# Attention output: the two halves of an accumulator added by GpSimd instead of VectorE

## The chip, the cores and the metric

The kernel runs on one core of a Trainium2 chip. The core has five engines that each run their own queue of instructions in order and wait for one another through semaphores: TensorE (PE; its weight loads are shown apart as PEld), VectorE (DVE), ScalarE (ACT), GpSimd (POOL) and SyncE (SP), which here issues DMAs. Matrix products land in PSUM; everything else lives in SBUF. The metric is the device time of one execution in microseconds (us).

## What is computed

An attention layer, a dense layer with a rational activation and a gated mixture of eight expert layers, one behind the other, in float32. Only the attention matters here:

```
B, H, S, D = q.shape                      # 2, 8, 768, 64
q_bits = (einsum('bhsd,dk->bhsk', q, proj) > 0)     # 6 bits; k_bits likewise
mask = q_bucket[:, :, :, None] == k_bucket[:, :, None, :]
scores = where(mask, q @ k.T / sqrt(D), -1e9)
attn = exp(scores - max) / (sum + 1e-9)
out = attn @ v                            # (b, s, h*64 + d) is the input of the next layer
```

## The kernel before

The program has an attention stage (to about 288 us), then the dense layer, then the experts. Precision is kept by splitting each float32 operand into a high half (rounded to the type that TensorE multiplies fast) and a low half, the rest; products are made of the halves.

The attention stage handles 16 heads (two batches of eight), each in three **groups** of 256 rows: 48 groups, `gi` from 0 to 47. The loop at the end of the listing runs over them with lags: in a turn it emits the scores of group `it`, the transposes of group `it - 2`, the products with v of group `it - 3`, and for a head's first two groups the preparation of the next head. Emission order is not the order of execution: a scheduler moves instructions within each engine's queue, by its own reckoning of what is ready, so every engine's order can change when one instruction changes. In a queue nothing overtakes.

The steps of a group, by name and line:

- `scores`: TensorE writes `s` (L277, L278); VectorE copies it to `e` and takes the row minimum of the negated scores (L285); ScalarE takes the exponential in place (L286).
- `norm`: VectorE makes the reciprocal row sums `rs` (L291, L292); GpSimd multiplies `e` by them, two tiles of 128x768 (L294). This is called the normalisation below.
- `trans`: TensorE transposes `e` into PSUM tiles `pt` (L308), which wait for L294; ScalarE copies them out as high halves `pth` (L106), VectorE makes the low halves `ptl` (L109).
- `values`: TensorE multiplies `pth` and `ptl` by `sv`, which holds v's high half in 64 columns and its low half in 64 more (L323). The accumulator `av` therefore has two halves in partitions 0 to 63 and 64 to 127 that must still be added. Before, ScalarE copies the lower one out to `avt`, and VectorE adds it to the upper one, read from PSUM, and writes 64 rows of `xp` (L334). `xp` collects two heads: an even head its rows 0 to 63, an odd head rows 64 to 127.
- Behind an odd head's group GpSimd splits 128x256 of `xp` into `xh` (L100) and `xl` (L103), the input of the dense layer.

For the next head GpSimd also splits v, q and k into `sv`, `sq`, `sk` (L100 and L103, 128x384 each); `sv` has three buffers. The tiles `av`, `pt`, `tp` and `hp` share four PSUM banks (tag "b"), so a bank must be read out before TensorE can use it again.

Beside attention the first weights of the dense layer are narrowed from 64-bit floats, eight of them in this stage. For one weight VectorE runs L180 to L183, GpSimd L170 (a clamp), L186 (an addition) and L103 (the low half, `wa` or `wb`), ScalarE L169 and a copy (L106) between L186 and L103.

Of the kernel before, what the change touches and what calls it, by code (L numbers as in the profile page):

```python
# [14 lines left out]
F32 = mybir.dt.float32  # L15
# [6 lines left out]
ALU = mybir.AluOpType  # L22
# [13 lines left out]
def kernel(  # L36
# [16 lines left out]
    pe, act, dve, pool, sp = nc.tensor, nc.scalar, nc.vector, nc.gpsimd, nc.sync  # L53
# [5 lines left out]
    P = 128  # L59
# [29 lines left out]
    def bank(name):  # L89
        return ps.tile([P, 512], F32, tag="b", bufs=4, name=name)  # L90
# [4 lines left out]
    def split(eng_hi, eng_lo, hi, lo, src):  # L95
        eng_hi(hi, src)
        eng_lo(lo, src, hi)
# [7 lines left out]
    def act_copy(o, src):  # L105
        act.activation(o, src, AF.Copy)  # L106
# [6 lines left out]
    ap = qkv_pool_stack.enter_context(tc.tile_pool(name="attn", bufs=2))  # L113
# [200 lines left out]
    def values(gi):  # L314
        i, g = divmod(gi, G)
        b, h = heads[i]
        sv = st[i][4]
        th, tl = pts.pop(gi)
        es.pop(gi)
        av = bank("av")  # L320
        for n, src in enumerate((th, tl)):
            for c in range(C):
                pe.matmul(av[:, 0:2 * P], lhsT=sv[:, c], rhs=src[:, c],  # L323
                          start=n == 0 and c == 0, stop=n == 1 and c == C - 1)
        if h % 2 == 0:
            if g == 0:
                xp[i] = ap.tile([P, S], F32, tag="xp", name="xp")
            x = xp[i]
        else:
            x = xp[i - 1]  # L330
        tmp = ap.tile([64, 2 * P], F32, tag="avt", name="avt")
        act_copy(tmp, av[64:128, 0:2 * P])
        r0 = (h % 2) * 64
        dve.tensor_tensor(x[r0:r0 + 64, g * 2 * P:(g + 1) * 2 * P], av[0:64, 0:2 * P], tmp, ALU.add)  # L334
        if h % 2:
            c0 = b * S + g * 2 * P
            tt, c0 = divmod(c0, 512)
            cs = slice(c0, c0 + 2 * P)
            split(pool_hi, pool_lo, xh[tt][:, h // 2, cs], xl[tt][:, h // 2, cs], x[:, g * 2 * P:(g + 1) * 2 * P])
# [381 lines left out]
    for it in range(NG + VLAG):  # L721
# [22 lines left out]
        i, g = divmod(it, G)  # L744
# [7 lines left out]
        if 0 <= vi < NG:  # L752
            values(vi)
# [183 lines left out]
```

## Time and profile before

| | us |
|---|---|
| three runs, median | 1613.9 |
| three runs, lowest and highest | 1613.78, 1615.29 |
| the profiled execution | 1613.6 |
| its span, first to last instruction | 1611.8 |

| engine | busy us, whole span | share |
|---|---|---|
| TensorE, matmul | 1549.2 | 96% |
| VectorE | 1224.9 | 76% |
| GpSimd | 930.0 | 58% |
| ScalarE | 621.0 | 39% |

The whole-span shares mix stages: in the attention stage VectorE, ScalarE and GpSimd are all much busier than later. So the stage is read alone, in stretches, and then by queue. The rows of a timeline give the start, the duration, the engine, the line, output and input; in square brackets stands the idle time of the engine just before, and what ended it. Matmul busy time includes time in which the pipeline drains.

### The profile page before, as it was taken

The numbers are of one execution on the slowest core, as the hardware profiler recorded it, in microseconds if no ns is written. First come the engines' busy times: TensorE is split into PE (matmuls) and PEld (weight loads), VectorE is DVE, ScalarE is ACT, GpSimd is POOL, SyncE is SP. The second block draws the span as 40 slices with busy tenths as digits, with TensorE's granted clock in tenths as the row PEclk, the third lists the DMA queues.
The fourth block names the chain that finished last, engine by engine and source line by source line (L and its number), as shares of the span: only waits on it lengthen the run. The fifth ranks groups of instructions, "written<-read, shape, count | busy, mean of one in ns | idle before, by whom it ended". The sixth has DMA issues, their size and how long they took to land.

```text
span 1611.8 us, 22139 instructions
## 1 busy us (share of the span) xinstructions
PE 1549.2 (96%) x8071; PEld 1354.4 (84%) x8071; DVE 1224.9 (76%) x2116; ACT 621.0 (39%) x1167; POOL 930.0 (58%) x1165
## 2 busy tenths in 40 slices
PE   5989999899999979999999999999999999999999
PEld 4888888777666868898989899898989989898987
DVE  7989989788999983786667767666766766676675
ACT  4888788787767833111111111111111111111111
POOL 7788785677777874456455345445534544553450
PEclk9999999999999989999999999999999999999999
DMA  5323220011111000011011001101100110110002
GB/s 168 86 81 90 69 76 15 27 53 61 57 53 66 1 26 27 27 40 40 27 34 45 27 27 40 40 27 38 42 27 27 40 40 27 39 40 27 27 1 78
DMA packets 49404, 71.83 MB, mean 45 GB/s; under 512 B 4368, under 2 KB 35088, under 8 KB 49296
## 3 DMA queue, kind: packets, MB, share of 16 engines
q1 hardware_dynamic: 48432, 68.85, 13.8%
q8 instruction: 64, 1.05, 0.3%
q10 hardware_dynamic: 864, 1.57, 0.3%
q14 instruction: 44, 0.36, 0.1%
HBM read 59.79 MB, written 3.15 MB: 39 GB/s over the span
## 4 chain that ended last, share of the span: by engine, by line
PE 71%; DVE 16%; ACT 5%; POOL 4%; issue 4%; DMA 1%; SPq 0%; POOLq 0%; DVEq 0%
PE accb L599 33%; PE prod L534 28%; PE av L323 2%; PE pt L308 2%; DVE tq L382 2%; DVE tu L384 2%; DVE tr L383 2%; POOL e L294 2%; PE acca L405 2%; PE h L354 1%; DVE e L285 1%; DVE bits L182 1%; DVE bits L180 1%; DVE tu L376 1%; DVE ptl L109 1%
## 5 line engine op out<-in xcount | busy, mean ns | idle before, releaser
L534 PE MATMUL prod<-xb,ww 128*128 128x384 f32 x2688 | 534.2, 337 | 5.7 <-DVE u L571 2.4
L534 PEld LDWEIGHTS prod<-xb,ww 128*128 128x128 f32 x2688 | 479.9, 189 | 40.7 <-ACT xb L106 2.9
L599 PE MATMUL accb<-wb,gh 128*128 128x512 f32 x1536 | 478.8, 393 | 0.0
L554 ACT ACTIVATE gh<-c 128x384 fp32r<-128x384 f32 x256 | 134.6, 526 | 764.5 <-DVE c L559 764.5
L610 DVE SCALAR_TENSOR_TENSOR osum<-accb,gp,osum 128x512 f32<-128x512 f32 x336 | 251.9, 750 | 208.3 <-PE accb L599 206.2
L599 PEld LDWEIGHTS accb<-wb,gh 128*128 128x128 f32 x1536 | 283.9, 188 | 36.4
L599 PE MATMUL accb<-wb,gl 128*128 128x512 f32 x768 | 305.9, 398 | 4.2 <-DVE gl L555 4.2
L100 POOL TENSOR_SCALAR ww<-ra 128x256 fp32r<-128x256 f32 x128 | 52.4, 410 | 407.9 <-PE prod L534 407.6
L555 DVE SCALAR_TENSOR_TENSOR gl<-c,gh 128x384 fp32r<-128x384 f32 x256 | 199.4, 779 | 4.5 <-ACT gh L554 4.3
L599 PEld LDWEIGHTS accb<-wb,gl 128*128 128x128 f32 x768 | 144.4, 188 | 35.1 <-DVE gl L555 4.6
L354 PE MATMUL h<-xh,wa 128*128 128x512 f32 x384 | 127.5, 395 | 5.8 <-DVE tu L377 5.6
L405 PE MATMUL acca<-gh,wb 128*128 128x512 f32 x384 | 128.0, 394 | 4.9 <-DVE part L417 2.6
L559 DVE TENSOR_TENSOR c<-prod,u 128x384 f32<-128x384 f32 x192 | 106.1, 552 | 27.2 <-PE prod L534 27.0
L109 DVE TENSOR_TENSOR ptl<-pt,pth 128x512 fp32r<-128x512 f32 x144 | 94.4, 681 | 19.0 <-ACT pth L106 18.2
L103 POOL TENSOR_TENSOR ww<-ra,ww 128x256 fp32r<-128x256 f32 x128 | 94.8, 740 | 10.7
L294 POOL TENSOR_SCALAR e<-e,rs 128x768 f32<-128x768 f32 x96 | 88.7, 934 | 19.6 <-DVE rs L292 10.1
L354 PEld LDWEIGHTS h<-xh,wa 128*128 128x128 f32 x384 | 72.1, 188 | 27.1 <-DVE tu L377 10.0
L405 PEld LDWEIGHTS acca<-gh,wb 128*128 128x128 f32 x384 | 72.1, 188 | 25.7 <-ACT gh L106 5.1
L285 DVE TENSOR_SCALAR_CACHE_REDUCE e<-s 128x768 f32<-128x768 f32 x96 | 90.8, 947 | 1.3 <-PE s L278 0.9
L308 PE MATMUL pt<-idr,e 128*128 128x128 f32 x576 | 81.3, 275 | 11.0 <-POOL e L294 4.7
L286 ACT ACTIVATE e<-e,nm 128x768 f32<-128x768 f32 x96 | 89.8, 935 | 3.5 <-DVE e L285 2.8
L103 POOL TENSOR_TENSOR wb<-rb,wb 128x512 fp32r<-128x512 f32 x64 | 84.3, 1317 | 5.3
(168 smaller groups left out, 2429.9 us busy)
## 6 DMA issues: line engine op xcount, KB each, us to landing
ra<-in_moe_w_dram SPq DMA_DIRECT2D x32, 512.0 KB
rb<-in_moe_w_dram SPq DMA_DIRECT2D x32, 512.0 KB
ra<-in_moe_w_in_dram SPq DMA_DIRECT2D x16, 512.0 KB
rb<-in_moe_w_out_dram SPq DMA_DIRECT2D x16, 512.0 KB
qkv<-in_q_dram SPq DMA_DIRECT2D x16, 192.0 KB
qkv<-in_k_dram SPq DMA_DIRECT2D x16, 192.0 KB
qkv<-in_v_dram SPq DMA_DIRECT2D x16, 192.0 KB
a<-a SPq DMA_DIRECT2D x16, 192.0 KB
```

Source lines behind the costliest of these rows:

```text
L103: pool.tensor_tensor(lo, src, hi.bitcast(F32), ALU.subtract)
L109: dve.tensor_tensor(lo, src, hi.bitcast(F32), ALU.subtract)
L285: dve.tensor_scalar(e[j], s[:, 0:S], BIG, None, ALU.min, ALU.min, accum_out=nm)
L294: pool.tensor_scalar(e[j], e[j], rs[:, j:j + 1], 0.0, ALU.mult, ALU.add)
L308: pe.transpose(pt[:, c, j * P:(j + 1) * P], e[j][:, cc * P:(cc + 1) * P], idf)
L354: pe.matmul(hps, lhsT=a[:, c], rhs=x[:, c], start=m == 0, stop=m == 3 * KC - 1)
L405: pe.matmul(o, lhsT=l[:, js], rhs=r, start=f == 0 and m == 0, stop=f == QF - 1 and m == 2)
L534: pe.matmul(o, lhsT=w[:, i, c], rhs=x[:, j, c], start=n == 0, stop=n == 5)
L554: act.activation(gh, c, AF.Relu)
L555: low.append(lambda: dve.scalar_tensor_tensor(gl, c, 0.0, gh.bitcast(F32), ALU.max, ALU.subtract))
L599: pe.matmul(o, lhsT=l[:, ts], rhs=r, start=f == 0 and m == 0, stop=f == 1 and m == 2)
L610: dve.scalar_tensor_tensor(d, o, gate["p"][:, n, e:e + 1], d, ALU.mult, ALU.add)
```

## The change

ScalarE copies both halves of the accumulator out, the upper one straight into `xp`, the lower one into `avt`, now in the same partitions as the rows of `xp`; GpSimd adds `avt` to `xp` in place. GpSimd cannot read PSUM, hence the second copy. VectorE's instruction is gone. Nothing else in the program text changes; `avt` takes 256 columns as before.

```diff
-        tmp = ap.tile([64, 2 * P], F32, tag="avt", name="avt")
+        rows = slice((h % 2) * 64, (h % 2) * 64 + 64)
+        xg = x[rows, g * 2 * P:(g + 1) * 2 * P]
+        tmp = ap.tile([P, 2 * P], F32, tag="avt", name="avt")[rows]
+        act_copy(xg, av[0:64, 0:2 * P])
         act_copy(tmp, av[64:128, 0:2 * P])
-        r0 = (h % 2) * 64
-        dve.tensor_tensor(x[r0:r0 + 64, g * 2 * P:(g + 1) * 2 * P], av[0:64, 0:2 * P], tmp, ALU.add)
+        pool.tensor_tensor(xg, xg, tmp, ALU.add)
```

The scheduler also moves other work. Three places, the lines as the programs have them (the new add is L336 there):

GpSimd inside an odd head of the first half, before: the normalisations, and the halves of `xp` of the head's first two groups between them.

```order
L294 TENSOR_SCALAR e<-e,rs 128x768 x2
L100 TENSOR_SCALAR xh<-xp 128x256
L103 TENSOR_TENSOR xl<-xp,xh 128x256
L294 TENSOR_SCALAR e<-e,rs 128x768 x2
L100 TENSOR_SCALAR xh<-xp 128x256
L103 TENSOR_TENSOR xl<-xp,xh 128x256
L100 TENSOR_SCALAR sv<-qkv 128x6x64
```

GpSimd at the same place of the changed program, head 3:

```order
L294 TENSOR_SCALAR e<-e,rs 128x768 x2
L186 TENSOR_TENSOR c<-rb 128x512
L336 TENSOR_TENSOR xp<-xp,avt 64x256
L100 TENSOR_SCALAR xh<-xp 128x256
L103 TENSOR_TENSOR xl<-xp,xh 128x256
L103 TENSOR_TENSOR wb<-c,wb 128x512
L294 TENSOR_SCALAR e<-e,rs 128x768 x2
L170 TENSOR_SCALAR c<-c 128x512
L336 TENSOR_TENSOR xp<-xp,avt 64x256
L100 TENSOR_SCALAR xh<-xp 128x256
L103 TENSOR_TENSOR xl<-xp,xh 128x256
L100 TENSOR_SCALAR sv<-qkv 128x6x64
```

Two adds stand between the normalisations and the halves, and a weight's L186 and L103 have moved here; the changed program narrows five weights in heads 1 to 5, one in each, where the one before spreads them over heads 3 to 10.

GpSimd where an odd head passes into an even one, late in the stage, before: from the normalisation behind `sv`, over the splits of q and k, to the next ones.

```order
L294 TENSOR_SCALAR e<-e,rs 128x768 x2
L100 TENSOR_SCALAR xh<-xp 128x256
L103 TENSOR_TENSOR xl<-xp,xh 128x256
L100 TENSOR_SCALAR sq<-qkv 128x6x64
L103 TENSOR_TENSOR sq<-qkv,sq 128x6x64
L100 TENSOR_SCALAR sk<-qkv 128x6x64
L103 TENSOR_TENSOR sk<-qkv,sk 128x6x64
L294 TENSOR_SCALAR e<-e,rs 128x768 x4
```

GpSimd at the same place of the changed program:

```order
L294 TENSOR_SCALAR e<-e,rs 128x768 x2
L336 TENSOR_TENSOR xp<-xp,avt 64x256
L100 TENSOR_SCALAR xh<-xp 128x256
L103 TENSOR_TENSOR xl<-xp,xh 128x256
L100 TENSOR_SCALAR sq<-qkv 128x6x64
L103 TENSOR_TENSOR sq<-qkv,sq 128x6x64
L100 TENSOR_SCALAR sk<-qkv 128x6x64
L103 TENSOR_TENSOR sk<-qkv,sk 128x6x64
L294 TENSOR_SCALAR e<-e,rs 128x768 x3
L336 TENSOR_TENSOR xp<-xp,avt 64x256
L294 TENSOR_SCALAR e<-e,rs 128x768
```

One add now stands ahead of the splits, and the first add of the next head between the two tiles of a normalisation.

ScalarE at one group's products, before:

```order
L106 ACTIVATE pth<-pt 128x512
L106 ACTIVATE avt<-av 64x256
L106 ACTIVATE pth<-pt 128x512 x2
L286 ACTIVATE e,rse<-e,nm 128x768
L106 ACTIVATE pth<-pt 128x512
```

ScalarE at the same place of the changed program:

```order
L106 ACTIVATE pth<-pt 128x512
L106 ACTIVATE xp<-av 64x256
L106 ACTIVATE avt<-av 64x256
L106 ACTIVATE pth<-pt 128x512 x2
L286 ACTIVATE e,rse<-e,nm 128x768
L106 ACTIVATE pth<-pt 128x512
```

The second copy stands right behind the first, ahead of the copies of the next transposes.

## Rows read from the trace of the kernel before

**Rows 1.** Stretches, head pairs: length, busy us (instructions) per engine, clock, DMA share, GB/s

```profile
core 0: us, PE busy (x) PEld busy (x) DVE busy (x) ACT busy (x) POOL busy (x), PEclk, DMA share, GB/s
...
58.26:89.19 30.93, 30.58 (x230) 28.06 (x231) 30.29 (x67) 25.36 (x55) 23.19 (x31) 1.00 0.26 70
89.19:125.07 35.88, 31.76 (x233) 28.63 (x232) 31.02 (x68) 28.74 (x61) 29.89 (x37) 1.00 0.31 89
125.07:159.08 34.01, 31.44 (x233) 28.62 (x232) 31.02 (x68) 27.53 (x59) 27.08 (x34) 1.00 0.28 79
159.08:192.01 32.93, 31.47 (x233) 28.62 (x232) 31.04 (x68) 26.87 (x58) 26.41 (x33) 1.00 0.29 81
192.01:224.48 32.47, 31.21 (x233) 28.36 (x232) 29.51 (x66) 26.82 (x58) 26.20 (x33) 1.00 0.29 83
224.48:255.14 30.66, 30.61 (x234) 28.05 (x233) 27.94 (x64) 26.41 (x57) 21.46 (x28) 1.00 0.14 32
```

**Rows 2.** TensorE's waits, 89 to 224 us: releaser, us in total, times, longest

```profile
PE pt L308 <- DVE ptl L109: 4.6, 7, 1.4
PE pt L308 <- POOL e L294: 3.2, 7, 0.6
PE av L323 <- DVE xp L334: 1.6, 3, 0.6
```

**Rows 3.** Timeline of GpSimd at a weight: start, us, instruction, idle before

```profile
133.75 0.51 POOL L100 TENSOR_SCALAR sv<-qkv 128x384 fp32r<-128x384 f32 x1 [0.76 <-PE av L323]
...
141.90 1.97 POOL L294 TENSOR_SCALAR e<-e,rs 128x768 f32<-128x768 f32 x2
143.84 1.03 POOL L186 TENSOR_TENSOR c<-rb 128x512 f32<-128x512 f32 x1
145.61 1.28 POOL L103 TENSOR_TENSOR wb<-c,wb 128x512 fp32r<-128x512 f32 x1 [0.74 <-ACT wb L106]
146.88 1.78 POOL L294 TENSOR_SCALAR e<-e,rs 128x768 f32<-128x768 f32 x2
```

**Rows 4.** Timeline of TensorE at two weights: transposes and products that wait

```profile
114.94 0.63 PE L308 MATMUL pt<-idr,e 128*128 128x128 f32 x4 [1.43 <-DVE ptl L109]
...
143.89 0.63 PE L308 MATMUL pt<-idr,e 128*128 128x128 f32 x4 [0.43 <-POOL e L294]
...
148.96 0.63 PE L308 MATMUL pt<-idr,e 128*128 128x128 f32 x4 [1.44 <-DVE ptl L109]
...
150.06 0.97 PE L323 MATMUL av<-pth,sv 128*128 128x256 f32 x6 [0.48 <-DVE xp L334]
```

**Rows 5.** Timeline of GpSimd in the pair without a weight

```profile
224.03 1.80 POOL L294 TENSOR_SCALAR e<-e,rs 128x768 f32<-128x768 f32 x2
225.81 0.40 POOL L100 TENSOR_SCALAR xh<-xp 128x256 fp32r<-128x256 f32 x1
...
227.61 1.79 POOL L294 TENSOR_SCALAR e<-e,rs 128x768 f32<-128x768 f32 x2 [0.58 <-DVE rs L292]
...
234.36 1.81 POOL L294 TENSOR_SCALAR e<-e,rs 128x768 f32<-128x768 f32 x2
...
240.50 1.80 POOL L294 TENSOR_SCALAR e<-e,rs 128x768 f32<-128x768 f32 x2
```

**Rows 6.** Timeline of TensorE there: the transposes that read those tiles

```profile
230.65 0.60 PE L308 MATMUL pt<-idr,e 128*128 128x128 f32 x4
...
242.34 0.63 PE L308 MATMUL pt<-idr,e 128*128 128x128 f32 x4
```

**Rows 7.** Groups of instructions, 0 to 450 us: count, busy us, mean ns, idle before

```profile
L334 DVE TENSOR_TENSOR xp<-av,avt 64x256 f32<-64x256 f32 x48 | 19.8, 412 | 1.7 <-ACT avt L106 1.0
...
L106 ACT ACTIVATE avt<-av 64x256 f32<-64x256 f32 x48 | 18.3, 381 | 20.3 <-PE av L323 19.8
...
L103 POOL TENSOR_TENSOR xl<-xp,xh 128x256 fp32r<-128x256 f32 x24 | 17.7, 736 | 2.0
...
L170 POOL TENSOR_SCALAR c<-c 128x512 f32<-128x512 f32 x24 | 14.9, 622 | 1.8 <-ACT c L169 1.2
```

## The prediction, on record before the changed kernel ran

> **What bounds the kernel now.** I read the busy time by stages first, then the waits of TensorE inside the stage that the change touches, then the queues of GpSimd and TensorE row by row. The change touches only the attention stage, up to about 288 us. I cut it into pairs of heads, each from the L334 of one odd head's first group to that of the next odd head; weights for the later stage are narrowed beside it. In the last pair no weight is narrowed, TensorE is busy for 30.61 of 30.66 us, and a pair costs 30.66 us: that is TensorE's own work, the floor [rows 1]. The five pairs before it cost 30.93, 35.88, 34.01, 32.93 and 32.47 us, which is 166.2 us where the floor is 153.3. So 12.9 us in all, 0.8% of the kernel, lie above the floor, and no change of copies can win more here. VectorE looks like the bound of these pairs (29.5 to 31.0 us busy, GpSimd 23.2 to 29.9), but a busy share is not a wait. TensorE's own waits between 89 and 224 us sum to 4.6 + 3.2 + 1.6 = 9.4 us [rows 2]. Look at one weight: GpSimd runs without idle from 133.75, except the 0.74 us before L103, through the weight's L186 and L103, to the normalisation that ends at 148.66 [rows 3], and TensorE waits 0.43, 1.44 and 0.48 us there [rows 4]. The page puts 1.44 down to ptl on VectorE, yet the transposes at 148.96 start 0.3 us after that normalisation ends. GpSimd's queue, not VectorE's time, holds this place.
>
> Without a weight the queue is still just in time: the normalisation of 240.50 ends at 242.30 [rows 5] and the transposes that read it start at 242.34 [rows 6]. The one of 227.61 ends at 229.40 and is needed at 230.65, 1.25 us later.
>
> **The change part by part.** Each of the 48 groups loses one VectorE add, 48 x 0.412 = 19.8 us, and gains one ScalarE copy of 64x256, 48 x 0.381 = 18.3 us [rows 7]. The GpSimd add of 64x256 is not in the trace. The nearest row is GpSimd's subtraction of 128x256, 0.736 us [rows 7]: the same number of columns, twice the partitions. Half the partitions may be cheaper, so the bounds are 0.41 us (VectorE's price for the add) and 0.80 us (0.736 stretched as a pair of normalisations is stretched from 1.80 to 1.97 us beside other work [rows 3, 5]). Below nothing is excluded: it is an instruction in a queue that runs in order. I take 0.736, the row of the same engine and length: 48 x 0.736 = 35.3 us more on GpSimd.
>
> The Trainium skill speaks against this move: "GPSIMD Engine Reference", section 4.1 Engine selection, gives two-input elementwise work to VectorE because GpSimd takes about twice as long. The rows give 0.736 / 0.412 = 1.8, near that. By the page an add would be an estimated 0.82 us and the sum below about 1 us higher.
>
> ScalarE's extra 0.381 us stands behind the first copy, ahead of the high halves (pth) of the next transposes; VectorE no longer has 0.412 us in its queue ahead of their low halves (ptl). On that way the two cancel, and I cost them at nothing. If ScalarE is late instead, each of its groups pays up to 0.38 us; ScalarE has 25.4 to 28.7 us of work per pair [rows 1] and gets 2.3 more, so it still has room. The accumulator bank is now freed by ScalarE alone: the 1.6 us of waits on L334 [rows 2] go.
>
> What counts is where the adds stand on GpSimd. Three kinds of place:
>
> A. A weight narrowed at the start of an even head. Two of the five weights stand there in the new order. Before, TensorE waits 0.43 + 1.44 + 0.48 = 2.35 us [rows 4]. Now one add more stands ahead of the normalisations in this unbroken run (+0.74; the other falls into the 0.74 us in which GpSimd waits for ScalarE), and the 0.48 us for L334 goes: 2.6 us, twice, 5.2 us.
>
> B. A weight narrowed inside an odd head. The new order has three of these, where before had one. From the row at 224.03, whose work ends at 225.83: add 0.74 (ahead of that normalisation), then L186 1.03, add 0.74, the two halves xh and xl 1.14 (0.40 and 0.736), L103 1.28, normalisation 1.79. That ends at 232.55, and TensorE wants it at 230.65 [rows 3, 5 to 7]: 1.9 us late, three times, 5.7 us. Without the two adds it would be 0.4 us.
>
> C. The crossing from an odd to an even head without a weight, four times. One add stands between the normalisation of 234.36 and that of 240.50. The slack there is 0.04 us, so it costs 0.7 us, four times, 2.8 us. The other adds of a head fall where GpSimd waits anyway: ahead of sv, which waits for the last product of a head on TensorE (0.76 us at 133.75 [rows 3]), and ahead of the next xh.
>
> The sum: 5.2 + 5.7 + 2.8 = 13.7 us of TensorE waits against 9.4 before, +4.3. Of the 4.6 us of waits on ptl two, 1.43 and 1.44, are such places at weights [rows 4] and not VectorE's; of the other 1.7 us I let 0.7 go with VectorE's lighter queue, a little under half, since GpSimd's queue stands behind part of them too. That leaves +3.6 us. On the profiled execution's 1613.6 us this is 1617.2; the median is 0.3 us above it, so 1617.5. Bounds of this case: against all 12.9 us above the floor instead of the waits that are seen, and with 0.7 us of relief, it is +0.1; with adds of 0.41 us (twelve of them stand in the three places) it is -0.3, with 0.80 us +4.4, and with the small waits repeated in the three new places B (12.9 / 9.4 = 1.37 times the 13.7, less 12.9, is +5.9, less 0.7) it is +5.2. So 1613.6 to 1619.1.
>
> **The rivals.** First, VectorE was the bound after all. For it: 29.5 to 31.0 us busy in every pair of 32.5 to 35.9 us [rows 1]. Each pair loses 6 x 0.412 = 2.5 us of it. Cut at each pair's excess over the floor (5.2, 3.4, 2.3, 1.8) that is 2.5 + 2.5 + 2.3 + 1.8 = 9.1 us at most; as GpSimd's normalisations hold about half of the waits, half of it, 4.5: 1609.4 us. Against it: the unbroken GpSimd run above.
>
> Second, slower by more: GpSimd becomes the bound of the heads that now carry a weight each. A pair with one weight has 27.1 us of GpSimd work [rows 1]; six adds and a second weight (L186 1.03, L103 1.28, L170 0.62 [rows 3, 7]) make it 34.4. In the row GpSimd idles 6.9 us of 34.01, because its queue waits for TensorE at sv; if half of that stays, such a pair costs 38 us. Two such pairs against 30.93 + 35.88 are +9.2 us, the third, with 31.5 + 3.5 against 34.01, is +1, and if the later pairs give nothing back it is 1624 us. It decides from the point at which GpSimd no longer idles ahead of sv.
>
> Third, nothing: the 6.9 us of idle time per pair take all 4.4 us of adds, and the five weights cost as before: 1614 us. For it, GpSimd idles 9.2 us in the pair of 224 to 255 us. Against it, that idle time lies ahead of sv and xh, not ahead of the late normalisation.
>
> **How the numbers follow.** The forecast, GpSimd's adds on the way to the normalisations, gets 0.45, half of it above +3.2 us, which is 0.2%, about what a measurement of this kernel can tell from no change. VectorE's relief gets 0.20 (0.15 faster, 0.05 within 0.2%), GpSimd as the bound 0.20, nothing 0.15. Faster is then 0.15, within 0.2% 0.22 + 0.05 + 0.15 = 0.42, slower 0.23 + 0.20 = 0.43. The likeliest case's own range is 1613.6 to 1619.1. The 8-in-10 range takes in VectorE's relief to a little past its half, 1608, and GpSimd as the bound to its price, 1625.
>
> **What would show it.** VectorE's busy time falls by 20 us, ScalarE's rises by 18, GpSimd's by 35. Right: TensorE's waits put down to e of L294 grow, those on xp are gone, and the pairs with two weights are the longest, at 33 us and more. The price is wrong if the adds do not take 0.7 us. Term C is wrong if the pairs without a weight stay at 30.7 us. VectorE was the bound if the pairs with weights fall under 32 us; GpSimd is if its idle time ahead of sv is gone there.

## The result and the profile after

| | us |
|---|---|
| changed kernel, median of 6 runs | 1625.67 |
| lowest and highest | 1625.33, 1626.45 |
| kernel before, median of 6 runs beside it | 1614.0 |
| ratio, with its 95% interval | 1.0069 [1.0056, 1.0082] |
| span of the profiled execution, before and after | 1611.8, 1623.4 |

The change costs 11.7 us; forecast were 3.6. Nearly all of it is lost inside the attention stage: the last head starts 11.3 us later than before. From here on a **head** is the time from one VectorE threshold (L260, which makes `bits` once per head) to the next. In the changed kernel the late heads, which carry no weight any more, take 16.1 us each; before, such heads take 15.2 to 15.4.

The page of the changed kernel: busy time with its share of the span, and one of its groups (columns as in [rows 7]).

```profile
PE 1554.4 (96%) x8071; PEld 1356.8 (84%) x8071; DVE 1209.6 (75%) x2068; ACT 636.8 (39%) x1215; POOL 964.4 (59%) x1213
L109 DVE TENSOR_TENSOR ptl<-pt,pth 128x512 fp32r<-128x512 f32 x144 | 95.7, 685 | 37.7 <-ACT pth L106 36.9
```

The same group on the page of the kernel before:

```profile
L109 DVE TENSOR_TENSOR ptl<-pt,pth 128x512 fp32r<-128x512 f32 x144 | 94.4, 681 | 19.0 <-ACT pth L106 18.2
```

VectorE lost 15 us of work and gained 19 us of waiting for ScalarE's `pth`. The engine that was relieved now stands and waits for the engine that was loaded. In the groups of the changed kernel between 30 and 310 us, the three instructions that replace the old pair (the first of them answers to L334 in [rows 7]):

```profile
L336 POOL TENSOR_TENSOR xp<-xp,avt 64x256 f32<-64x256 f32 x48 | 36.2, 755 | 9.2 <-ACT avt L106 7.8
L106 ACT ACTIVATE avt<-av 64x256 f32<-64x256 f32 x48 | 18.3, 380 | 1.0
L106 ACT ACTIVATE xp<-av 64x256 f32<-64x256 f32 x48 | 18.0, 376 | 14.8 <-PE av L323 14.1
```

TensorE's waits in the stage (30 to 310 us), as in [rows 2]: releaser, us in total, times, longest:

```profile
PE pt L308 <- POOL e L294: 6.4, 10, 1.5
PE tp L245 <- DVE ptl L109: 6.0, 12, 0.7
PE pt L308 <- DVE ptl L109: 5.9, 4, 3.7
```

The second line is the new one: in 12 heads the transposes of the next head's keys (`tp`, L245) wait half a microsecond for `ptl`; the kernel before has two such waits, 1.5 us in all. The old waits for `xp` of L334 are gone. The third line holds one long wait, in the head in which the first moved weight is narrowed. The timeline of ScalarE, VectorE and TensorE there:

```profile
62.03 0.63 ACT L106 ACTIVATE wb<-c 128x512 fp32r<-128x512 f32 x1 [1.90 <-POOL c L186]
67.03 0.66 ACT L169 ACTIVATE c<-rb 128x512 f32<-128x512 f32 x1 [3.45 <-POOL wb L103]
67.60 0.58 ACT L106 ACTIVATE pth<-pt 128x512 fp32r<-128x512 f32 x1
68.21 0.69 DVE L109 TENSOR_TENSOR ptl<-pt,pth 128x512 fp32r<-128x512 f32 x1 [4.53 <-ACT pth L106]
69.05 0.63 PE L308 MATMUL pt<-idr,e 128*128 128x128 f32 x4 [3.70 <-DVE ptl L109]
69.43 1.21 PE L323 MATMUL av<-pth,sv 128*128 128x256 f32 x6
```

GpSimd runs from 58.35 to 67.0 us without idle time here, with an add, `xh` and `xl` in between. ScalarE's L169 needs the buffer that GpSimd's L103 frees; `pth` stands behind it in ScalarE's queue, `ptl` waits for `pth`, and TensorE for `ptl`. Each releaser is an engine further up; the start of the chain is GpSimd's length. And the wait costs more than its 3.70 us. Three stretches of that place (the third lies within the second), columns as in [rows 1]:

```profile
65.00:70.00 5.00, 1.30 (x11) 1.06 (x10) 1.79 (x4) 2.90 (x7) 3.41 (x5) 1.00 0.08 15
70.00:75.00 5.00, 5.00 (x26) 4.59 (x25) 4.30 (x11) 4.24 (x10) 3.89 (x7) 0.66 0.06 10
70.60:74.00 3.40, 3.40 (x17) 3.21 (x16) 2.73 (x7) 2.66 (x7) 2.46 (x4) 0.50 0.00 0
```

TensorE on either side of the wait:

```profile
64.07 1.04 PE L308 MATMUL pt<-idr,e 128*128 128x128 f32 x8
72.93 1.57 PE L308 MATMUL pt<-idr,e 128*128 128x128 f32 x8
```

The granted clock is 1.00 up to the wait and 0.66 on average between 70 and 75 us, because it stands at 0.50, the lower of the two levels (1.2 and 2.4 GHz), from 70.6 to 74.0 us. Eight transposes take 1.57 us there, where the same eight took 1.04 us before the wait.

### The profile page after: what moved, and what is told of

It is laid out like the page before. It is cut to its first block, busy times and chain, and to the rows that moved or that the text cites. A ratio compares the mean times of both kernels' runs of the same rounds, so it can differ in the third digit from the quotient of the medians.

```text
span 1623.4 us, 22253 instructions
## 1 busy us (share of the span) xinstructions
PE 1554.4 (96%) x8071; PEld 1356.8 (84%) x8071; DVE 1209.6 (75%) x2068; ACT 636.8 (39%) x1215; POOL 964.4 (59%) x1213
## 3 DMA queue, kind: packets, MB, share of 16 engines
q10 hardware_dynamic: 864, 1.57, 0.3%
## 4 chain that ended last, share of the span: by engine, by line
PE 71%; DVE 13%; ACT 5%; POOL 5%; issue 3%; DMA 0%; DVEq 0%; POOLq 0%
PE accb L601 33%; PE prod L536 28%; PE av L323 2%; PE pt L308 2%; POOL e L294 2%; DVE tq L384 2%; DVE tu L386 2%; DVE tr L385 2%; PE acca L407 2%; PE h L356 1%; DVE ptl L109 1%; DVE bits L182 1%; DVE bits L180 1%; DVE tu L378 1%; ACT e L286 1%
## 5 line engine op out<-in xcount | busy, mean ns | idle before, releaser
L109 DVE TENSOR_TENSOR ptl<-pt,pth 128x512 fp32r<-128x512 f32 x144 | 95.7, 685 | 37.7 <-ACT pth L106 36.9
L103 POOL TENSOR_TENSOR ww<-ra,ww 128x256 fp32r<-128x256 f32 x128 | 95.1, 743 | 10.7
L294 POOL TENSOR_SCALAR e<-e,rs 128x768 f32<-128x768 f32 x96 | 89.0, 938 | 13.3 <-DVE rs L292 9.4
L356 PEld LDWEIGHTS h<-xh,wa 128*128 128x128 f32 x384 | 72.1, 188 | 27.2 <-DVE tu L379 10.2
L286 ACT ACTIVATE e<-e,nm 128x768 f32<-128x768 f32 x96 | 90.3, 940 | 4.2 <-DVE e L285 4.1
L103 POOL TENSOR_TENSOR wb<-rb,wb 128x512 fp32r<-128x512 f32 x64 | 84.1, 1315 | 5.3
```

The source lines that it names most:

```text
L103: pool.tensor_tensor(lo, src, hi.bitcast(F32), ALU.subtract)
L109: dve.tensor_tensor(lo, src, hi.bitcast(F32), ALU.subtract)
L286: act.activation(e[j], e[j], AF.Exp, bias=nm, scale=-1.0, accum_out=rs[:, j, 0:1])
L294: pool.tensor_scalar(e[j], e[j], rs[:, j:j + 1], 0.0, ALU.mult, ALU.add)
L356: pe.matmul(hps, lhsT=a[:, c], rhs=x[:, c], start=m == 0, stop=m == 3 * KC - 1)
```

## The experiments

**Theories at the outset.** A: the loss comes from where the scheduler put the five weights (their L186 stand behind the normalisations of 6, 9, 12, 15 and 17 groups instead of 12, 15, 21, 27 and 33). B, called Q in the later runs: GpSimd's queue is too long by its adds. The first four runs try A and the parts of the change alone; S, that ScalarE's second copy lengthens every head, came out of them.

**gated.** The changed kernel; five weights are held back by a value that VectorE computes late.

```diff
-        pool.tensor_scalar(c, c, F64_HIGH, F64_LOW, ALU.min, ALU.max)
+        pool.tensor_scalar(c, c, high, F64_LOW, ALU.min, ALU.max)   # high: F64_HIGH, made from rs of group 9, 12, 18, 24, 30
```

> The change, with the five weights held back to the groups at which the kernel before narrows them (a tiny VectorE instruction per weight gates the clamp on GpSimd). Theory A (the loss of heads 1 to 4 comes from the weights that the scheduler moved there: ScalarE stands behind GpSimd's late weight steps): the 9 us of heads 1 and 2 go, 1615 to 1620 us. Rival B (GpSimd's 48 adds stand ahead of the normalisations, wherever the weights are): 1622 to 1626 us.

Measured: 1627.11 us, ratio 1.0074 [1.0059, 1.0089]. The weights are back in the old groups and nothing is won: theory A falls. Heads without a weight still take 16.1 us.

**pool_alone.** The add on GpSimd, the upper half copied by VectorE.

```diff
-        act_copy(xg, av[0:64, 0:2 * P])
+        dve.tensor_copy(xg, av[0:64, 0:2 * P])
```

> The add on GpSimd as in the change, but the upper half is copied out by VectorE instead of ScalarE: GpSimd's 36 us more, ScalarE's and VectorE's work as before. Theory A with ScalarE as the late engine in heads without a weight: those heads back at 15.3 to 15.6 us, weights no worse than before, 1612 to 1616 us. Rival B: 1620 us and more.

**act_alone.** Both copies on ScalarE, the add on VectorE.

```diff
-        pool.tensor_tensor(xg, xg, tmp, ALU.add)
+        dve.tensor_tensor(xg, xg, tmp, ALU.add)
```

> ScalarE copies both halves as in the change, VectorE adds them from SBUF: ScalarE's 18 us more without GpSimd's 36. Theory A: heads without a weight cost 15.8 to 16.1 us as in the change, weights cost as before or less, 1616 to 1621 us. Rival B: no add on GpSimd, so 1612 to 1615 us.

Measured: 1627.71 us (1.0079 [1.0064, 1.0094]) and 1626.18 us (1.0068 [1.0052, 1.0085]). Each half alone costs as much as both, so the two don't add up, and these two runs don't divide the loss: neither is a clean half. Their heads without a weight take 16.0 us (pool_alone) and 16.0 to 16.2 us (act_alone), as long as those of the change. VectorE's group in pool_alone:

```profile
L334 DVE COPY xp<-av 64x256 f32<-64x256 f32 x48 | 19.9, 414 | 4.4 <-PE av L323 3.3
```

And in act_alone:

```profile
L336 DVE TENSOR_TENSOR xp<-xp,avt 64x256 f32<-64x256 f32 x48 | 32.9, 686 | 3.9 <-ACT avt L106 2.8
```

VectorE's plain copy takes 414 ns, as long as the add that it replaces [rows 7], so pool_alone relieves nobody. And an add with both operands in SBUF takes VectorE 686 ns on average, so act_alone loads VectorE by 13 us more.

The long heads of pool_alone need a word, since ScalarE copies only once there. GpSimd in one of them, columns as in [rows 1]:

```profile
237.35:253.40 16.05, 15.43 (x116) 13.71 (x114) 14.39 (x33) 13.33 (x28) 14.36 (x21) 1.00 0.13 31
```

From the add at 240.81 us to the end of a normalisation at 253.32 us GpSimd runs without a break (add, `xh`, `xl`, `sv`, normalisation, add, `xh`, `xl`, `sq`, `sk`, normalisation), and the chain that the profile follows through the head stays on GpSimd all that time; the transposes on TensorE start at its end. In this order GpSimd's queue, with two of the adds in it, sets the length of 16.0 us. A head of this length is therefore no sign of ScalarE's second copy by itself.

**no_add.** The changed kernel without the add; the lower half of the products is left out.

```diff
-        pool.tensor_tensor(xg, xg, tmp, ALU.add)
```

> The change without its add: both copies by ScalarE, nothing adds the halves (the output leaves out the lower half). Order on TensorE and places of the weights are those of the change. Theory A: the weights still stand in heads 1 to 5 but GpSimd is earlier by its adds, heads without a weight stay at 15.9 to 16.1 us; 1616 to 1621 us. Rival B: without the adds 1612 us or less.

Measured: 1617.71 us, ratio 1.0017 [1.0008, 1.0026]. The add is worth 8 us (1625.7 less 1617.7), but the rest of the change, which only takes an add from VectorE and gives a copy to ScalarE, still costs 2.6 against the kernel before measured beside it (1615.1). Its heads without a weight stay at 16.0 us.

**more_pool.** The kernel before plus one GpSimd add per group that nothing depends on. The weights stay in the groups of before.

```diff
+        more = ap.tile([64, 2 * P], F32, tag="more", name="more")
+        pool.tensor_tensor(more, tmp, tmp, ALU.add)
```

> The kernel before, with its VectorE add kept, and in each of the 48 groups one more GpSimd add of 64x256 that reads the copy of the lower half and writes a scratch tile that nobody reads. The weights stand in the same groups as in the kernel before (12, 15, 21, 27, 33). Theory Q (GpSimd's queue alone: 0.74 us more ahead of each normalisation) expects that TensorE's waits for L294 grow and that the time goes up by 6 us or more, as 1620 to 1626. Theory R (the adds cost where the data depend on them: the chain copy, add, splits behind ScalarE) expects less than 4 us, as 1614 to 1618, since nothing waits for this add but the queue.

Measured: 1625.94 us, ratio 1.0066 [1.005, 1.0083]. An add whose result nobody reads costs 11.8 us, by its place in GpSimd's queue (ScalarE's copy to `avt` waits for GpSimd only once in the stage, 1.5 us, so the buffer that the add reads isn't the cause). Its heads without a weight take 15.2 to 15.7 us late in the stage, as before; its heads with one take 17.9 to 20.9 us where before has 16.8 to 18.0. Timelines at one weight, GpSimd, ScalarE and TensorE:

```profile
149.44 0.92 POOL L294 TENSOR_SCALAR e<-e,rs 128x768 f32<-128x768 f32 x1
150.31 0.62 POOL L336 TENSOR_TENSOR more<-avt 64x256 f32<-64x256 f32 x1
150.88 1.05 POOL L186 TENSOR_TENSOR c<-rb 128x512 f32<-128x512 f32 x1
152.68 1.28 POOL L103 TENSOR_TENSOR wb<-c,wb 128x512 fp32r<-128x512 f32 x1 [0.74 <-ACT wb L106]
153.94 1.78 POOL L294 TENSOR_SCALAR e<-e,rs 128x768 f32<-128x768 f32 x2
...
151.97 0.63 ACT L106 ACTIVATE wb<-c 128x512 fp32r<-128x512 f32 x1 [3.54 <-POOL c L186]
...
156.02 0.63 PE L308 MATMUL pt<-idr,e 128*128 128x128 f32 x4 [2.06 <-DVE ptl L109]
157.13 1.23 PE L323 MATMUL av<-pth,sv 128*128 128x256 f32 x6 [0.48 <-DVE xp L334]
```

The add stands ahead of L186, so ScalarE's copy of the weight waits 3.54 us, with exponentials and high halves behind it; L103 stands ahead of the next normalisation, and TensorE waits 2.06 us where the kernel before waits 1.4 at such a place [rows 4]. Behind it six products take 1.23 us, where six at 151.03 us took 0.88. This is the prediction's own mechanism, at more than its price: the forecast held 4.3 us of additional waits for the adds in all (13.7 less 9.4). A part of the excess is TensorE's clock, granted at 0.50 in three stretches of 3.4 us (from 99.6, 120.1 and 157.7 us), where the kernel before has 1.00 throughout [rows 1].

**more_act.** The kernel before plus a second ScalarE copy per group that nobody reads.

```diff
         act_copy(tmp, av[64:128, 0:2 * P])
+        act_copy(more, av[0:64, 0:2 * P])
```

> The kernel before, with its VectorE add kept, and in each of the 48 groups a second ScalarE copy of 64x256, from the upper half of the accumulator into a scratch tile that nobody reads. No work on GpSimd is added. Theory S (ScalarE's 0.38 us ahead of the next high halves is what lengthens every head by 0.6 to 0.7 us) expects 48 groups at about 0.2 us, so +8 to +11 us over the kernel before, 1622 to 1625, heads without a weight at 16.0 us instead of 15.4, and VectorE's waits for pth grown from 18 us to more than 30. Theory T (the 0.38 us are hidden, and the heads are longer through the order that the scheduler makes) expects under 4 us.

Measured: 1617.87 us, ratio 1.002 [1.001, 1.0029]. The last three heads take 15.55, 15.80 and 15.55 us. Here S falls short: in this order, and with VectorE's add in place, the copy costs some 0.35 us per head (31.35 us in the last pair against 30.66), and VectorE's idle time ahead of `ptl` falls to 13.8 us where S expected more than 30.

**one_copy.** The changed kernel with one ScalarE copy per group, no second copy and no add (the lower half of the products is left out).

```diff
-        act_copy(tmp, av[64:128, 0:2 * P])
-        pool.tensor_tensor(xg, xg, tmp, ALU.add)
```

> The changed kernel with the add and the copy of the lower half both left out: one ScalarE copy of the upper half straight into xp per group, nothing on VectorE or GpSimd. It leaves out the lower half of the products. Against the run without the add it takes away one ScalarE copy per group. Theory S expects that heads without a weight fall back from 16.0 to 15.4 us and the time to 1607 to 1611, below the kernel before since 48 VectorE adds are gone as well. Theory T expects that the heads stay at 16.0 us and the time at 1615 to 1618.

Measured: 1615.67 us, ratio 1.0009 [1.0, 1.0018]. The heads without a weight are back at 15.4 us, as S expects, but the total isn't: two weights stand close together (L186 at 71.5 and 78.0 us), and the two heads from 77.4 us on take 22.2 us each. The weights' places make the totals of such runs hard to compare. So the next ones leave the weights out.

**late_copies.** The changed kernel with the copies and the add written behind the turn's last transposes, so that `pth` goes first on ScalarE.

```diff
-            values(vi)
+            rest = values(vi)          # products only
             ...
             trans(ti, 1)
             trans(ti, 2)
+        if 0 <= vi < NG:
+            rest()                     # the two copies, the add, the split
```

> The changed kernel with the same instructions, but with the two ScalarE copies and the GpSimd add written behind the last two transposes of the turn instead of ahead of them, so that the scheduler ranks pth above the copies. Theory S expects that VectorE's waits for pth fall from 37 us and the time by 4 to 8 us, 1618 to 1622. Theory Q expects the time to stay within 3 us of the changed kernel, since GpSimd's queue is as long.

Measured: 1624.71 us, ratio 1.0067 [1.0052, 1.0082]. The heads without a weight take 15.9 and 16.5 us in turn, and `tp` still waits for `ptl`, 13 times. Putting `pth` ahead wins next to nothing. Two things grow beside it: the accumulator's bank is read out 1.53 us after a group's last product where the changed kernel takes 1.27 (mean of groups 27 to 44), and TensorE's waits for GpSimd's normalisation go from 6.4 to 10.0 us. Which of them eats the gain isn't shown.

**before_now and after_now.** Both kernels without the narrowing of the five weights; a copied weight stands in, so the dense layer's products differ.

```diff
+        if one and 2 < m + 2 * i < 2 * QF:
+            for k in range(2):
+                sp.dma_start(slots[m, i][k].bitcast(F32), slots[m, 0][k].bitcast(F32))
+            load_weights(m, c + 2)
+            return
```

> The kernel before without the narrowing of the same five weights, in the same way. Its heads without a weight take 15.4 us, and the other heads lie 13.3 us above that, so about 1601 is expected by every theory. The difference to the changed kernel without the weights is what tells: Theory S expects some 9.5 us of the 11.7, Theory Q expects 2 us or less.

> The changed kernel without the narrowing of the five weights that stand in the heads: a copied weight is put in their place by DMA, so the products of the dense layer are not the reference's. What is left is the price of the change in a head without a weight. Theory S (the second ScalarE copy lengthens every head without a weight to 16.1 us) expects heads of 16.1 us throughout and, since the heads with weights of the changed kernel lie 15.1 us above that, about 1610.5. Theory Q (GpSimd's queue, at weights alone) expects heads near 15.4 us and 1602 or less.

Measured: 1600.47 and 1610.36 us. So 9.9 us of the change's loss have nothing to do with the weights, and the weights cost 14.0 us before (1614.5 less 1600.5) and 15.3 us after (1625.7 less 1610.4). Below are the timelines of ScalarE, VectorE and TensorE where one head passes into the next, of before_now:

```profile
203.76 0.38 ACT L106 ACTIVATE avt<-av 64x256 f32<-64x256 f32 x1 [0.53 <-PE av L328]
204.04 0.92 ACT L291 ACTIVATE e<-e,nm 128x768 f32<-128x768 f32 x1
205.08 1.09 ACT L106 ACTIVATE pth<-pt 128x512 fp32r<-128x512 f32 x2
205.71 1.29 DVE L109 TENSOR_TENSOR ptl<-pt,pth 128x512 fp32r<-128x512 f32 x2
206.86 0.46 PE L250 MATMUL tp<-idr,sk 128*128 128x128 f32 x4
```

And of after_now, where the same transposes wait 0.57 us:

```profile
209.15 1.29 DVE L109 TENSOR_TENSOR ptl<-pt,pth 128x512 fp32r<-128x512 f32 x2 [0.58 <-ACT pth L106]
211.34 0.95 ACT L291 ACTIVATE e<-e,nm 128x768 f32<-128x768 f32 x1 [0.34 <-DVE e L290]
212.28 0.36 ACT L106 ACTIVATE xp<-av 64x256 f32<-64x256 f32 x1
212.67 0.38 ACT L106 ACTIVATE avt<-av 64x256 f32<-64x256 f32 x1
213.07 0.60 ACT L106 ACTIVATE pth<-pt 128x512 fp32r<-128x512 f32 x1
213.71 0.69 DVE L109 TENSOR_TENSOR ptl<-pt,pth 128x512 fp32r<-128x512 f32 x1 [0.80 <-ACT pth L106]
214.46 0.54 PE L250 MATMUL tp<-idr,sk 128*128 128x128 f32 x4 [0.57 <-DVE ptl L109]
```

It is a chain, and every head runs through it once: `ptl` waits for `pth`, the exponential for `e` behind that `ptl`, the two copies for the exponential, the next `pth` for the copies, its `ptl` for that, and TensorE for the bank that `ptl` frees. No instruction in it is slow. The chain that the profile follows through this head agrees: between 209.75 and 214.46 us it runs over just these instructions and not over TensorE, while in the head of before_now from 198.51 us it never leaves TensorE. TensorE is idle for 0.6 us of each head. (L250, L291 and L328 here are L245, L286 and L323 of the kernel before.)

**t1.** after_now with the transposes of the keys written behind the second half of the scores, since in before_now two score products stand between those of the queries and those of the keys, and in after_now none.

```diff
             scores(it, 1)
+        if half:
+            list(half)                 # transposes of sk, split off prep_head_a
```

> The changed kernel without the five weights (a copied weight in their place, as in the run without the weights), and with the transposes of the next head's keys written behind the second half of the scores, so that TensorE no longer has them right behind those of the queries. The instructions are the same. If the order on TensorE is the cause, heads fall from 16.1 to 15.4 to 15.6 us and the time from 1610.4 to 1600 to 1604. If ScalarE's time or the accumulator's bank is, the wait moves to another place and the time stays at 1608 to 1612.

Measured: 1610.25 us, heads of 16.0 us. TensorE's order isn't the cause. The wait moved. TensorE's waits from 60 to 255 us in after_now:

```profile
PE tp L250 <- DVE ptl L109: 7.5, 12, 0.7
```

And in t1, ahead of the transposes of `e`:

```profile
PE pt L317 <- DVE ptl L109: 5.8, 12, 0.7
```

**after_t1.** The same edit in the whole changed kernel.

> The changed kernel with all its weights and the order of t1: nothing left out. If the order is the cause of the 0.75 us per head, some 9 us come back and it ends at 1615 to 1619, near the kernel before; otherwise 1623 to 1627.

Measured: 1627.19 us, ratio 1.0074 [1.0059, 1.009], and so nothing is won there either.

**noadd_now, sbuf_now, one_now.** after_now, taken apart; all three leave out the lower half of the products. noadd_now drops the add. sbuf_now also lets the second copy read the first one in SBUF, so that it costs ScalarE's time but no longer holds the accumulator's bank. one_now drops the second copy.

```diff
# noadd_now
-        pool.tensor_tensor(xg, xg, tmp, ALU.add)
# sbuf_now, besides
-        act_copy(tmp, av[64:128, 0:2 * P])
+        act_copy(tmp, xg)
# one_now, in place of that
-        act_copy(tmp, av[64:128, 0:2 * P])
```

> The changed kernel without the five weights (a copied weight in their place) and without the GpSimd add, both ScalarE copies from the accumulator kept; it leaves out the lower half of the products. If the second copy is the price of a head without a weight, heads stay at 16.0 us and the time is 1608 to 1610. If the add is, heads fall to 15.4 us and the time to about 1600.

> The changed kernel without the five weights and without the GpSimd add, and with the second ScalarE copy reading the first copy in SBUF and not the accumulator, so that the accumulator's bank is free after the first copy; it leaves out the lower half of the products too. TensorE's order at the crossing stays as in the changed kernel. With both copies from the accumulator and no add, heads without a weight took 16.0 us; with one copy 15.4. If the bank is the cause, heads fall to 15.4 and the time to about 1600; if ScalarE's time is, they stay at 15.9 to 16.1 and the time is about 1608.

> The same with the second ScalarE copy left out as well: one copy of the upper half per group, no add. If ScalarE's copy and the bank it holds are the price, heads take 15.4 us, as in the kernel before, and the time is 1599 to 1601. If it is something else in the changed program, 1604 or more.

Eleven heads without a weight in the five kernels, from one L260 to the eleventh after it, one stretch of each kernel, columns as in [rows 1]. before_now:

```profile
75.83:244.44 168.61, 168.32 (x1278) 154.28 (x1277) 153.65 (x352) 145.25 (x308) 123.91 (x160) 1.00 0.24 64
```

after_now, ScalarE 10 us and GpSimd 24 us busier, TensorE idle for 6.8 us:

```profile
76.88:254.02 177.14, 170.31 (x1280) 155.42 (x1279) 143.49 (x319) 155.45 (x341) 147.79 (x194) 1.00 0.23 60
```

noadd_now, where TensorE is idle for 6.6 us still:

```profile
77.14:253.07 175.93, 169.36 (x1279) 155.17 (x1278) 143.64 (x320) 155.45 (x341) 123.36 (x161) 1.00 0.23 61
```

sbuf_now, with as much work on ScalarE, TensorE idle for 2.0 us:

```profile
76.10:248.78 172.68, 170.72 (x1279) 155.24 (x1277) 145.93 (x320) 155.03 (x340) 123.50 (x161) 1.00 0.24 62
```

one_now, where TensorE has no idle time to speak of:

```profile
74.64:243.97 169.33, 168.92 (x1281) 155.85 (x1280) 143.19 (x320) 141.02 (x309) 122.81 (x160) 1.00 0.23 64
```

| kernel, all without the five weights | us | a head | next step down |
|---|---|---|---|
| after_now | 1610.36 | 16.10 | add on GpSimd: 1.6 |
| noadd_now | 1608.79 | 15.99 | second copy reads SBUF, not the bank: 4.3 |
| sbuf_now | 1604.50 | 15.70 | second copy left out: 6.2 |
| one_now | 1598.26 | 15.39 | |
| before_now | 1600.47 | 15.33 | |

From one_now up to noadd_now the second copy costs 10.5 us for 18.3 us of work. VectorE's relief by 48 adds is worth at most 2.2 us (one_now against before_now, which also frees the bank sooner), and none of it in these eleven heads: TensorE is at its floor in both. How long VectorE stands idle ahead of `ptl` follows the second copy, in one_now and then in noadd_now:

```profile
L109 DVE TENSOR_TENSOR ptl<-pt,pth 128x512 fp32r<-128x512 f32 x144 | 93.5, 683 | 8.7 <-ACT pth L106 7.8
L109 DVE TENSOR_TENSOR ptl<-pt,pth 128x512 fp32r<-128x512 f32 x144 | 96.1, 686 | 36.5 <-ACT pth L106 35.5
```

Two reservations stay with the division into bank and time. In sbuf_now the scheduler also put the second copy behind a `pth` in some groups, so 4.3 and 6.2 are sizes for this order. And the bank's time alone doesn't make a head long: from a group's last product to the end of the last copy or add that reads the bank (mean of groups 27 to 44) it is 1.26 us in noadd_now and 0.84 in sbuf_now, but 1.36 in before_now, whose heads are the shortest.

**after_hi and before_hi.** In both kernels the copy that makes a weight's high half goes to GpSimd, so that ScalarE's queue never waits for L186.

```diff
-            act_copy(t[:, 0], n)
+            pool_hi(t[:, 0], n)        # in the attention stage only
```

> The changed kernel, with the high halves of the weights narrowed in this stage (a copy of 128x512 between the addition L186 and the low half L103) made by GpSimd itself and no longer by ScalarE. GpSimd no longer stands idle 0.74 us there, but has some 0.62 us more to do; ScalarE's queue never waits for GpSimd's addition. Theory P (what a weight costs is ScalarE's queue, which stands still behind the late GpSimd addition with the exponentials and high halves of attention behind it) expects a gain of 4 us or more, 1618 to 1622. Theory Q (GpSimd's length alone) expects no gain, 1624 to 1628.

> The kernel before with the same edit on the weights' high halves. Theory P expects 1609 to 1612, since the heads with weights lie 13.3 us above those without and a part of it is ScalarE's wait. Theory Q expects 1613 to 1617.

Measured: 1633.7 us (1.0117 [1.0102, 1.0133]) and 1619.2 us (1.0025 [1.0015, 1.0034]). The theory that ScalarE's wait for L186 is what a weight costs is not borne out: that wait is gone and both kernels are slower. The test isn't a clean one, though. A part of ScalarE's waiting for GpSimd (17.5 and 20.2 us for L186) only moved to L169 (10.2 us in after_hi where the changed kernel has 5.3, 11.6 in before_hi where the kernel before has 1.9), and the edit takes in the three weights of the first heads, where before_hi loses 3.6 of the 5.4 us by which its last head is late. That GpSimd's 0.62 us more per weight are dearer than ScalarE's wait was speaks for Q, at a price that Q had not foreseen.

**before_wb.** The kernel before, with three of the five weights narrowed in the first steps of the dense layer.

```diff
-            for m in range(2):
+            for m in range(2 if wprep[it] == 0 else 1):
             ...
+    for j in range(1, QF):
+        prep_at(j - 1, 1, j)
```

> The kernel before, with three of the five weights that are narrowed in the heads (wb for the second to fourth block) narrowed in the first three steps of the dense layer instead, where their products come six steps later. A weight costs 2.7 us in a head (the five cost 1614.5 - 1600.5 = 14 us); three of them are 8 us. If the dense layer has room beside its products, 1606 to 1609; if it is as full as the heads, 1612 to 1617.

Measured: 1614.35 us, ratio 0.9997 [0.9987, 1.0006]. The eighth to the last head take 15.2 to 15.5 us as hoped, and the stage ends some 7 us earlier. But the dense layer gives it all back. TensorE's waits from 255 to 400 us:

```profile
PE h L354 <- DVE tu L377: 9.5, 4, 4.4
```

Against 3.0 us for the same wait before. So no version was found that beats the kernel before.

## Why the prediction was wrong

**The floor and the way of reading: right.** Two kernels without weights run at 15.3 and 15.4 us per head, twice that is the floor of [rows 1], and TensorE is busy for 168.3 of 168.6 us. That GpSimd's queue, and not VectorE's time, holds the places at weights was right too: more_pool shows it without any change of data flow.

**The price of the add: right.** 0.736 us forecast, 0.755 measured on average (44 of the 48 take 0.72 to 0.74).

**"On that way the two cancel, and I cost them at nothing": the step that failed.** It set ScalarE's 0.381 us against VectorE's 0.412 us because both lie between `pth` and `ptl`. Measured in the kernels without the five weights, the new copy costs 10.5 us (0.6 us per head) and the VectorE add gives back at most 2.2. Two things were overlooked. VectorE had idle time anyway (19 us ahead of `ptl` on the page before), so removing its add only made it idle longer: 26.1 us of the eleven heads in one_now against 15.0 in before_now, most of it ahead of `e`. And ScalarE's copies stand ahead of a `pth` for which VectorE was already waiting: with the second one the idle time ahead of `ptl` goes from 8.7 to 36.5 us. The prediction had the right alternative at hand ("each of its groups pays up to 0.38 us"), which is 18 us at most, but called ScalarE roomy by its busy share, 25.4 to 28.7 us in a pair of 31 to 36, after having said itself that a busy share is not a wait. The row that would have told was VectorE's idle time ahead of L109, put down to `pth`.

**"The accumulator bank is now freed by ScalarE alone: the 1.6 us of waits on L334 go": half right.** Those waits went. But two copies in a row keep the bank nearly as long as the old copy and add did (1.26 us in noadd_now, 1.36 in before_now, as above), and in the changed order that is not free: letting the second copy read SBUF instead is worth 4.3 us.

**Terms A and B, the weights: net right by luck, gross wrong.** Forecast 10.9 us against 9.4, so +1.5; measured 15.3 against 14.0, +1.3: both sizes were too small, by 4.4 and 4.6 us, and the errors cancel. In the changed kernel a part of it is slower work behind a wait (granted clock 0.66 from 70 to 75 us and 0.81 from 105 to 110), which no row of waits contains. In the kernel before the clock is 1.00 throughout; there TensorE's busy time lies above the floor, by 3.4 us in the five pairs [rows 1], and the waits don't contain that either. And the net hides a trade: with VectorE's add gone but no GpSimd add, the weights cost 8.9 us (no_add less noadd_now); the adds bring them back to 15.3. That this relief is VectorE's is not shown, since the weights' places move too.

**Term C: the place wrong, the size near.** It put 0.7 us on four crossings from an odd to an even head, 2.8 us in all, by the add on GpSimd. In after_now the adds cost 1.6 us in heads without a weight, and what grew there by 0.75 us was every head, odd or even; most of that goes when the second copy goes. (In the order of pool_alone GpSimd's queue does hold such heads, as the term had it.) The test that the prediction gave for this term ("wrong if the pairs without a weight stay at 30.7 us") would have called it right, as those pairs go to 32.2 us: a length alone doesn't tell which engine made it. The other signs were met as well: TensorE's waits for `e` of L294 grew from 4.7 to 6.4 us, those for `xp` of L334 went, and the pairs with two weights are the longest, at 39.3 and 37.5 us (cut as in the prediction). None of them could show the copy.

**The sum by what was measured:** -2.2 + 6.2 + 4.3 + 1.6 + 1.3 = 11.2 us, against 11.7. (The terms are differences between the same medians, so that they add up proves nothing; the 0.5 us is the kernel before, at 1614.0 and at 1614.5.) The forecast held 2.8 - 0.7 + 1.5 = 3.6. All but a little of the difference is the copy. **The rival at 1624 us** (GpSimd as the bound) came near in time, and its sign is met in part: ahead of `sv` GpSimd idles for 0.78, 1.49, 0.09, 1.42 and 0 us in the five heads with a weight. But most of the loss has another reason: 9.9 us are lost without these weights, where GpSimd idles ahead of `sv` in every head and is busy for 147.8 of 177.1 us in after_now.

**What stays open:** why the same second copy costs only 3.7 us in all in more_act, with VectorE's idle time ahead of `ptl` at 13.8 us. VectorE keeps its add there, and the scheduler's order is another. TensorE's order was tried (t1) and isn't it; the order on ScalarE was tried only together with the time that the bank is held (late_copies), that on VectorE not at all. So 10.5 us is the price of the copy in the changed kernel's order, and a part of it may be the order's.

## What to carry to other kernels

When four engines pass one tile around in a loop that is full, the price of moving work is not its time on the engine that has room, but what stands behind it in that engine's queue and who already waits for that: look up the idle time that names the receiving engine as its releaser before you call it roomy. A second reader of a PSUM bank can cost more than its own time: letting the second copy read SBUF instead was worth 4.3 us here. And taking work from an engine that is waiting for others gives little back: 19.8 us of VectorE's work were worth at most 2.2.

## What the runs showed of the hardware that was not expected

VectorE's add of 64x256 with one operand in PSUM takes 0.41 us at every place [rows 7]. With both operands in SBUF (act_alone) it takes 0.41 to 1.27 us, depending on what GpSimd does at the time. Timelines of VectorE and GpSimd in act_alone:

```profile
224.60 0.41 DVE L336 TENSOR_TENSOR xp<-xp,avt 64x256 f32<-64x256 f32 x1
227.77 0.98 DVE L336 TENSOR_TENSOR xp<-xp,avt 64x256 f32<-64x256 f32 x1
...
222.67 1.80 POOL L294 TENSOR_SCALAR e<-e,rs 128x768 f32<-128x768 f32 x2 [1.92 <-DVE rs L292]
...
227.46 1.01 POOL L103 TENSOR_TENSOR sv<-qkv,sv 128x384 fp32r<-128x384 f32 x1
```

At 224.60 the last GpSimd work of the stretch has ended (at 224.47) and the add takes its plain time; at 227.77 it runs beside GpSimd's subtraction and ends 0.28 us after that does. So it is at nearly all such places: of the 31 adds that take more than 0.43 us, 29 end 0.27 to 0.28 us behind the end of a GpSimd instruction, and the 14 beside which GpSimd does nothing take 0.41 to 0.42 us.

GpSimd's add takes 0.607 us on average where both operands are the same tile (more_pool) and 0.72 to 0.74 us, in 44 of 48 of the changed kernel, where they are two. VectorE's copy of 64x256 out of PSUM takes as long as an add of that size, 0.414 us.
